# Banded attention feeding a token mixer on one core: a bias table multiplied in after exp, global keys batched over heads, and the attention of one batch interleaved with the mixing of another

## The chip, the core and the metric

The kernel runs on one core of one Trainium2 chip. The time is device microseconds (us) of one execution; a result is the median of several executions. The engines are PE (TensorE: matmuls and transposes), PEld (its weight loads, which overlap PE), DVE (VectorE), ACT (ScalarE: exp, sin and copies), POOL (GpSimd, which here also issues the input DMAs) and SP (which issues the output DMAs). Slow executions (over 1.5% above the fastest of the same kernel) are in the medians and ranges below, but not in the ratios. A verdict against the kernel before is a ratio: the mean time of one kernel's fast runs over the mean of the other's fast runs of the same rounds on the same chip. It is therefore not quite the ratio of the medians that are quoted beside it.

## The reference

There are 4 batches, 8 heads, 768 positions, head size 64. Attention is banded: a query sees the 96 keys up to and including its own position, and the first 8 keys of the sequence ("global keys"). A linear distance penalty is added to the scores. Then a token mixer works on the 768 x 512 result of each batch.

```python
# attention, for each batch b and head h
scores = q @ k.T / sqrt(64)
rel    = pos_q - pos_k
local  = (rel >= 0) & (rel < 96)
glob   = pos_k < 8
dist   = where(glob & ~local, 96, abs(rel))
scores = where(local | glob, scores - slope[h] * dist, -1e9)
x[b, :, h*64:(h+1)*64] = softmax(scores) @ v

# mixer, for each batch (x is 768 x 512)
theta = x @ w_theta                                    # "theta stretch"
y = w_tok_r @ (x * cos(theta)) + w_tok_i @ (x * sin(theta))   # "mixing"
u = x + y
out = u + relu(u @ w_ch)                               # "channel"
```

Mixing is the largest piece. It is 72 matmuls of 512 columns a batch; theta and channel are 24 each.

## The kernel before

Scores are computed transposed, keys on the partitions, in blocks of 128 keys by 256 queries, so exp gives directly what the value matmul needs as its stationary operand. The softmax sum comes from a column of ones beside v. The distance penalty and the mask are put into PSUM by a matmul of the identity with a bias table, and the scores are accumulated on top. Each head pair's q is copied into two tiles that are zero in the other head's 64 rows, so that a full 128-row matmul gives one head's scores.

```python
qTz_pool = [...]                       # per head of a pair: [128, 768], other head's rows zeroed
# per head:
for pair_i, jts in enumerate(((0, 1), (2, 3), (4, 5))):
    nc.tensor.matmul(ps_sc[...], lhsT=ident, rhs=biasM_all[h][:, b0:b0 + ncols, :],   # L195
                     start=True, stop=False)
    for sub, jt in enumerate(jts):
        nc.tensor.matmul(ps_sc[:, sub, 0:n * T], lhsT=kT2[:, jt * T:(jt + 1) * T],     # L203
                         rhs=qTz[:, its[0] * T:(its[-1] + 1) * T], start=False, ...)
nc.tensor.matmul(ps_gl[0:NG, :], lhsT=kT2[:, 0:NG], rhs=qTz[:, 2 * T:S], ...)          # L210 global keys
# [...]
nc.scalar.activation(exp_sb[...], ps_scs[hh][pair_i][...], AF.Exp, scale=scale)        # L220
nc.scalar.activation(eg[0:NG, :], ps_gls[hh][0:NG, :], AF.Exp, scale=scale, bias=...)  # L227
# [...] value matmuls L243: 128 x 128 by 128 x 65
```

The order of work leaves two batches of mixing for the end:

```python
for b in (0, 1):                       # attention alone
    # [...] attention_pair(b, 0), (b, 2), (b, 4), (b, 6), with the weight set-up in batch 0
for b in (2, 3):                       # attention of b beside the mixer of b - 2
    attention_pair(b, 0); moe_stage1(b - 2)            # theta
    attention_pair(b, 2); moe_stage2(b - 2, (0, 1, 2)) # mixing, L289
    attention_pair(b, 4); moe_stage2(b - 2, (3, 4, 5))
    attention_pair(b, 6); moe_stage3(b - 2)            # channel, L308
moe_stage1(2); moe_stage1(3); moe_stage2(2, ...); moe_stage2(3, ...)   # [...] the last two, alone
```

The softmax here doesn't subtract the row's maximum and nothing guards it: scores larger than these inputs give would overflow.

Of the kernel before, what the change touches and what calls it, by code (L numbers as in the profile page):

```python
# [9 lines left out]
FP = mybir.dt.float32  # L11
# [6 lines left out]
def kernel(  # L18
# [18 lines left out]
    NC = DM // T  # L37
    NG = int(n_global)
    NL = int(n_local)
    scale = 1.0 / math.sqrt(D)  # L40
    INF = 30000.0
    slopes = [2.0 ** (-8.0 * (h + 1) / H) for h in range(H)]
    HALF_PI = math.pi / 2.0

    const = ctx.enter_context(tc.tile_pool(name="const", bufs=1))
    xpool = ctx.enter_context(tc.tile_pool(name="xpool", bufs=2))
    abuf = ctx.enter_context(tc.tile_pool(name="abuf", bufs=3))
    mbuf = ctx.enter_context(tc.tile_pool(name="mbuf", bufs=2))
    psum = ctx.enter_context(tc.tile_pool(name="psum", bufs=8, space=bass.MemoryType.PSUM))

    def ps_tile(shape, dtype):
        return psum.tile(shape, dtype, name="ps", tag="ps")

    blk = {}
    nblk = 0
    for jt in range(NT):
        for it in ([0, 1] if jt == 0 else [i_ for i_ in (jt, jt + 1) if i_ < NT]):
            blk[(jt, it)] = nblk
            nblk += 1
# [3 lines left out]
    prefetch_requests = [(0, 0), (0, 2)]  # L63

    bias_glob = const.tile([T, H], FP)
    for h in range(H):
        nc.gpsimd.memset(bias_glob[:, h:h + 1], -float(NL) * slopes[h])
    halfpi = const.tile([T, 1], FP)
    nc.gpsimd.memset(halfpi, HALF_PI)

    dist_diag = const.tile([T, T], FP)
    nc.gpsimd.iota(dist_diag, pattern=[[1, T]], base=0, channel_multiplier=-1,
                   allow_small_or_imprecise_dtypes=True)
    nc.gpsimd.affine_select(dist_diag, dist_diag, pattern=[[1, T]], base=0,
                            channel_multiplier=-1, compare_op=ALU.is_ge, fill=INF)
    nc.gpsimd.affine_select(dist_diag, dist_diag, pattern=[[-1, T]], base=NL - 1,
                            channel_multiplier=1, compare_op=ALU.is_ge, fill=INF)

    dist_super = const.tile([T, T], FP)
    nc.gpsimd.iota(dist_super, pattern=[[1, T]], base=T, channel_multiplier=-1,  # L80
                   allow_small_or_imprecise_dtypes=True)
    nc.gpsimd.affine_select(dist_super, dist_super, pattern=[[-1, T]], base=NL - 1 - T,
                            channel_multiplier=1, compare_op=ALU.is_ge, fill=INF)

    g_row = const.tile([T, T], FP)
    nc.gpsimd.memset(g_row, float(NL))
    nc.gpsimd.affine_select(g_row, g_row, pattern=[[0, T]], base=NG - 1,
                            channel_multiplier=-1, compare_op=ALU.is_ge, fill=INF)

    dist_diag0 = const.tile([T, T], FP)  # L90
    nc.vector.tensor_tensor(dist_diag0, dist_diag, g_row, op=ALU.min)
    dist_super0 = const.tile([T, T], FP)
    nc.vector.tensor_tensor(dist_super0, dist_super, g_row, op=ALU.min)

    biasM_all = []
    for h in range(H):
        e_t = const.tile([T, 11, T], BF, name=f"biasM_all_{h}")
        f = -slopes[h] / scale
        nc.scalar.mul(e_t[:, 0, :], dist_diag0, f)
        nc.scalar.mul(e_t[:, 1, :], dist_super0, f)  # L100
        nc.scalar.mul(e_t[:, 2:11:2, :], dist_diag[:, None, :].to_broadcast([T, 5, T]), f)
        nc.scalar.mul(e_t[:, 3:10:2, :], dist_super[:, None, :].to_broadcast([T, 4, T]), f)
        biasM_all.append(e_t)

    eg_tiles = []
    for i_ in range(4):
        egt = const.tile([T, 4 * T], BF, name=f"eg_{i_}")
        nc.vector.memset(egt, 0.0)
        eg_tiles.append(egt)
    eg_cnt = [0]  # L110

    qTz_pool = [[], []]
    for hh in range(2):
        for i_ in range(3):
            t_ = const.tile([T, S], BF, name=f"qTz_{hh}_{i_}")
            nc.vector.memset(t_, 0.0)
            qTz_pool[hh].append(t_)
    qTz_cnt = [0, 0]

    w_theta_bf = const.tile([T, NC, DM], BF)  # L120
    w_ch_bf = const.tile([T, NC, DM], BF)
    w_tokT = [const.tile([T, NT, S], BF, name=f"w_tokT_{wi}") for wi in range(2)]
    w_nats = {}

    def setup_wsmall():
        nc.gpsimd.dma_start(out=w_theta_bf, in_=moe_w_theta.rearrange("(c p) n -> p c n", p=T))
        nc.gpsimd.dma_start(out=w_ch_bf, in_=moe_w_ch.rearrange("(c p) n -> p c n", p=T))
        for wi, w_src in enumerate((moe_w_tok_r, moe_w_tok_i)):
            w_nat = mbuf.tile([T, NT, S], BF, name="w_nat", bufs=2)
            nc.gpsimd.dma_start(out=w_nat, in_=w_src.rearrange("(c p) n -> p c n", p=T))  # L130
            w_nats[wi] = w_nat

    def setup_wtok(wi):
        w_nat = w_nats[wi]
        wT = w_tokT[wi]
        for st in range(NT):
            ps_tr = ps_tile([T, S], BF)
            for tt in range(NT):
                nc.tensor.transpose(ps_tr[:, tt * T:(tt + 1) * T],
                                    w_nat[:, tt, st * T:(st + 1) * T], ident)  # L140
            nc.vector.tensor_copy(out=wT[:, st, :], in_=ps_tr)

    x_sb = {}

    def load_pair(b, h0):
        qp = abuf.tile([T, NT, 2 * D], BF, name="qp")
        kp = abuf.tile([T, NT, 2 * D], BF, name="kp")
        for src, dst in ((q, qp), (k, kp)):
            for hh in range(2):
                nc.gpsimd.dma_start(  # L150
                    out=dst[:, :, hh * D:(hh + 1) * D],
                    in_=src[b, h0 + hh].rearrange("(t p) d -> p t d", p=T))
        v1s = []
        for hh in range(2):
            v1 = abuf.tile([T, NT, D + 1], BF, name=f"v1_{hh}")
            nc.gpsimd.dma_start(out=v1[:, :, 0:D],
                                in_=v[b, h0 + hh].rearrange("(t p) d -> p t d", p=T))
            nc.gpsimd.memset(v1[:, :, D:D + 1], 1.0)
            v1s.append(v1)
        return qp, kp, v1s  # L160

    preloaded = {}

    def attention_pair(b, h0):
        if (b, h0) in preloaded:
            qp, kp, v1s = preloaded.pop((b, h0))
        else:
            qp, kp, v1s = load_pair(b, h0)

        ps_q = ps_tile([T, S], BF)  # L170
        ps_k = ps_tile([T, S], BF)
        for src, pst in ((qp, ps_q), (kp, ps_k)):
            for t_ in range(NT):
                nc.tensor.transpose(pst[:, t_ * T:(t_ + 1) * T], src[:, t_, :], ident)  # L174
        qTzs = []
        for hh in range(2):
            t_ = qTz_pool[hh][qTz_cnt[hh] % 3]
            qTz_cnt[hh] += 1
            R = slice(D * hh, D * (hh + 1))
            nc.vector.tensor_copy(out=t_[R, :], in_=ps_q[R, :])  # L180
            qTzs.append(t_)
        kT2 = abuf.tile([T, S], BF, name="kT2")
        nc.scalar.copy(out=kT2, in_=ps_k)

        exp_sbs, ps_scs, ps_gls, egs = [], [], [], []
        for hh in range(2):
            h = h0 + hh
            qTz = qTzs[hh]
            exp_sbs.append(abuf.tile([T, 11, T], BF, name="exp_sb"))
            banks = []  # L190
            for pair_i, jts in enumerate(((0, 1), (2, 3), (4, 5))):
                ncols = 4 if pair_i < 2 else 3
                b0 = blk[(jts[0], 0 if jts[0] == 0 else jts[0])]
                ps_sc = ps_tile([T, 2, 2 * T], FP)
                nc.tensor.matmul(  # L195
                    ps_sc.rearrange("p a b -> p (a b)")[:, 0:ncols * T],
                    lhsT=ident,
                    rhs=biasM_all[h][:, b0:b0 + ncols, :].rearrange("p a b -> p (a b)"),
                    start=True, stop=False)
                for sub, jt in enumerate(jts):  # L200
                    its = [0, 1] if jt == 0 else [i_ for i_ in (jt, jt + 1) if i_ < NT]
                    n = len(its)
                    nc.tensor.matmul(ps_sc[:, sub, 0:n * T],  # L203
                                     lhsT=kT2[:, jt * T:(jt + 1) * T],
                                     rhs=qTz[:, its[0] * T:(its[-1] + 1) * T],
                                     start=False, stop=(sub == len(jts) - 1))
                banks.append(ps_sc)
# [23 lines left out]
        for hh in range(2):  # L231
# [3 lines left out]
            for it in range(NT):  # L235
                mms = []
                if it >= 2:
                    mms.append((eg[:, (it - 2) * T:(it - 1) * T], v1[:, 0, :]))
# [80 lines left out]
    for b in (0, 1):  # L319
        x_sb[b] = xpool.tile([T, NT, DM], BF, name="x_sb", bufs=4)  # L320
        attention_pair(b, 0)
        if b == 0:
            setup_wsmall()
# [61 lines left out]
```

## Time and profile before

Before the prediction the time was 255.59 us (254.84 to 257.77, 3 runs).

| | before |
|---|---|
| span of the profiled run | 255.4 us |
| PE busy, idle | 208.8 us, 46.6 us (the difference) |
| DVE, ACT, POOL busy | 114.9, 121.8, 87.7 us |
| share of PE in the chain of waits | 55% |

From the profile page of the kernel before: the span, the busy time of each engine, PE's busy tenths in 40 equal slices (6.4 us each), and the shares of the chain of work that ended last.

```profile
span 255.4 us, 4349 instructions
PE 208.8 (82%) x1712; PEld 118.7 (46%) x1736; DVE 114.9 (45%) x248; ACT 121.8 (48%) x230; POOL 87.7 (34%) x154
PE   0439819899868949999999759999999999999950
PE 55%; DMA 12%; POOL 9%; ACT 9%; DVE 8%; issue 5%; DVEq 0%; POOLq 0%; ACTq 0%
```

PE is nearly full from the middle on. It is thin in the first twelve slices, has a dip where theta is computed (the "75" in the middle is one), and is empty in the last slice.

The busy time of each engine by stretch of time (start:end, length, then busy time and number of instructions of PE, PEld, DVE, ACT and POOL, the granted clock, DMA share and GB/s):

```profile
82.00:94.00 12.00, 8.22 (x76) 4.88 (x75) 8.34 (x20) 8.61 (x15) 9.73 (x15) 1.00 1.25 80
138.00:149.00 11.00, 7.27 (x56) 3.98 (x57) 7.80 (x20) 8.14 (x14) 1.27 (x4) 1.00 0.62 62
201.00:232.00 31.00, 30.84 (x143) 14.06 (x144) 11.82 (x22) 5.26 (x10) 0.00 (x0) 1.00 0.00 1
```

The first two are theta stretches of batches 0 and 1: PE is busy 8.2 of 12 and 7.3 of 11 us. The third is mixing of the last two batches, alone: PE is full, and the other engines have little to do. That is the room that the change wants to use.

Groups of instructions before (line, engine, operation, output and inputs, shapes, count, then busy time and mean ns of one, then idle time before them):

```profile
L289 PE MATMUL ps<-zri,w_tokT_170 128*128 128x512 bf16 x142 | 53.8, 379 | 0.3
L220 ACT ACTIVATE exp_sb<-ps 128x512 bf16<-128x512 f32 x64 | 34.3, 583 | 10.0 <-PE ps L203 9.9
L273 DVE TENSOR_TENSOR zri<-x_sb,cs 128x512 bf16<-128x512 bf16 x24 | 10.1, 421 | 5.3 <-ACT cs L271 5.1
```

The 379 ns of a mixing matmul is the duration of one; matmuls overlap in the pipeline. What one costs in a row is read from the chain of waits, which gives start, length and count:

```profile
208.18 10.74 PE ps L289 x49
```

That is 10.74 / 49 = 0.219 us for a matmul of 512 columns.

### The profile page before, as it was taken

The page shows a single profiled execution, that of the slowest core. Times are in us where ns is not written, and L with a number is a line of the kernel's source. Part 1 is how long each engine was busy: PE and PEld are TensorE (multiplying, and loading weights), DVE is VectorE, ACT ScalarE, POOL GpSimd, SP SyncE. Part 2 cuts the span into 40 slices and gives each one's busy share as a digit, 9 for nine tenths or more (in the row PEclk, how much of TensorE's full clock was granted, in tenths as well). Part 3 has the DMA queues.
Part 4 walks back from the last instruction along what each step waited for, and adds up shares of the span by engine and source line. Part 5 has one row for each costly group of instructions (what it writes and reads, how often), then busy time and mean ns, then how long its engine had stood idle before and what let it go on. Part 6 is the DMA issues. An engine that isn't in the chain of part 4 may idle for free.

```text
span 255.4 us, 4349 instructions
## 1 busy us (share of the span) xinstructions
PE 208.8 (82%) x1712; PEld 118.7 (46%) x1736; DVE 114.9 (45%) x248; ACT 121.8 (48%) x230; POOL 87.7 (34%) x154
## 2 busy tenths in 40 slices
PE   0439819899868949999999759999999999999950
PEld 0216616666646525454646325555655444445520
DVE  5103432555423562323566533333678752325742
ACT  6985607598858585161618792332609730000000
POOL 9985128959566675571625000000000000000000
PEclk9999988999989997999999979999999999999995
DMA  4999999999899996993959300000042000000444
GB/s 27 115 129 195 211 163 92 110 87 99 55 77 85 92 84 41 92 74 21 78 141 197 22 0 0 3 0 0 3 166 85 0 0 0 3 0 0 164 167 164
DMA packets 81364, 19.42 MB, mean 76 GB/s; under 512 B 75712, under 2 KB 78272, under 8 KB 81344
## 3 DMA queue, kind: packets, MB, share of 16 engines
q0 software_dynamic: 77888, 12.85, 66.4%
q1 hardware_dynamic: 3456, 6.29, 6.7%
q8 instruction: 14, 0.23, 0.4%
q14 instruction: 6, 0.05, 0.1%
HBM read 25.69 MB, written 6.29 MB: 125 GB/s over the span
## 4 chain that ended last, share of the span: by engine, by line
PE 55%; DMA 12%; POOL 9%; ACT 9%; DVE 8%; issue 5%; DVEq 0%; POOLq 0%; ACTq 0%
PE ps L289 24%; PE ps L267 8%; DMA kp<-in_k_dram 7%; PE ps L203 5%; PE ps L243 4%; DMA out_dram<-o_sb 4%; ACT exp_sb L220 4%; PE ps L308 4%; PE ps L195 3%; DVE o_sb L312 3%; POOL kp L150 3%; PE ps L174 3%; POOL qp L150 3%; PE ps L210 2%; DMA v_0_190<-in_v_dram 1%
## 5 line engine op out<-in xcount | busy, mean ns | idle before, releaser
L289 PE MATMUL ps<-zri,w_tokT_170 128*128 128x512 bf16 x142 | 53.8, 379 | 0.3
L289 PE MATMUL ps<-zri,w_tokT_171 128*128 128x512 bf16 x139 | 52.7, 379 | 0.1
L220 ACT ACTIVATE exp_sb<-ps 128x512 bf16<-128x512 f32 (+1 forms) x96 | 46.5, 550 | 10.0 <-PE ps L203 9.9
L250 DVE RECIPROCAL rec<-ps 128x6 f32<-128x6 f32 x32 | 6.2, 194 | 65.7 <-PE ps L243 65.5
L293 DVE TENSOR_TENSOR u<-x_sb,ps 128x512 bf16<-128x512 bf16 x24 | 16.5, 687 | 36.3 <-PE ps L289 34.4
L150 POOL DMA_DIRECT2D qp<-in_q_dram x32 | 26.6, 841 | 14.3 <-PE ps L174 4.7
L150 POOL DMA_DIRECT2D kp<-in_k_dram x32 | 27.0, 853 | 0.9 <-PE ps L174 0.4
L271 ACT ACTIVATE cs<-ps,halfpi 128x512 bf16<-128x512 f32 x24 | 16.9, 703 | 16.4 <-PE ps L267 14.2
L312 DVE SCALAR_TENSOR_TENSOR o_sb<-ps,u 128x512 f32<-128x512 f32 x24 | 16.1, 687 | 13.9 <-DMA out_dram<-o_sb 11.6
L267 PE MATMUL ps<-w_theta_bf,xT 128*128 128x512 bf16 x92 | 21.5, 379 | 0.6 <-DVE xT L262 0.3
L308 PE MATMUL ps<-w_ch_bf,uT 128*128 128x512 bf16 x92 | 21.4, 379 | 0.3
L289 PEld LDWEIGHTS <-w_tokT_170 128*128 128x128 bf16 x144 | 14.1, 98 | 16.1
L289 PEld LDWEIGHTS <-w_tokT_171 128*128 128x128 bf16 x144 | 14.1, 98 | 16.1
L243 PEld LDWEIGHTS <-exp_sb 128*128 128x128 bf16 x352 | 17.6, 100 | 8.3 <-ACT exp_sb L220 2.3
L251 DVE TENSOR_TENSOR x_sb<-ps,rec 128x384 bf16<-128x384 f32 x32 | 17.8, 555 | 0.9
L174 PE MATMUL ps<-ident,qp 128*128 128x128 bf16 x96 | 8.5, 228 | 11.7 <-DMA qp<-in_q_dram 11.7
L272 ACT ACTIVATE cs<-ps 128x512 bf16<-128x512 f32 x24 | 14.7, 614 | 0.0
L267 PEld LDWEIGHTS <-xT 128*128 128x128 bf16 x96 | 9.0, 98 | 11.3 <-DVE xT L262 2.2
L308 PEld LDWEIGHTS <-uT 128*128 128x128 bf16 x96 | 8.9, 98 | 11.0 <-DVE uT L303 1.9
L174 PEld LDWEIGHTS <-qp 128*128 128x128 bf16 x96 | 6.5, 102 | 13.5 <-issue 7.2
L273 DVE TENSOR_TENSOR zri<-x_sb,cs 128x512 bf16<-128x512 bf16 x24 | 10.1, 421 | 5.3 <-ACT cs L271 5.1
L195 PEld LDWEIGHTS <-ident 128*128 128x128 bf16 x96 | 9.4, 105 | 6.3 <-issue 4.6
(341 smaller groups left out, 348.8 us busy)
## 6 DMA issues: line engine op xcount, KB each, us to landing
out_dram<-o_sb SPq DMA_DIRECT2D x24, 256.0 KB, 2.0
qp<-in_q_dram POOLq DMA_DIRECT2D x32, 96.0 KB, 3.4
kp<-in_k_dram POOLq DMA_DIRECT2D x32, 96.0 KB, 3.4
w_nat<-in_moe_w_tok_r_dram POOLq DMA_DIRECT2D x1, 1152.0 KB, 13.2
w_nat<-in_moe_w_tok_i_dram POOLq DMA_DIRECT2D x1, 1152.0 KB, 18.1
w_theta_bf<-in_moe_w_theta_dram POOLq DMA_DIRECT2D x1, 512.0 KB, 7.5
w_ch_bf<-in_moe_w_ch_dram POOLq DMA_DIRECT2D x1, 512.0 KB, 8.5
v_0_178<-in_v_dram POOLq DMA_DIRECT2D x1, 96.0 KB, 3.6
```

Of the source, the lines that this page charges most:

```text
L150: nc.gpsimd.dma_start(out=dst[:, :, hh * D:(hh + 1) * D], in_=src[b, h0 + hh].rearrange("(t p) d -> p t d", p=T))
L174: nc.tensor.transpose(pst[:, t_ * T:(t_ + 1) * T], src[:, t_, :], ident)
L195: nc.tensor.matmul(ps_sc.rearrange("p a b -> p (a b)")[:, 0:ncols * T], lhsT=ident, rhs=biasM_all[h][:, b0:b0 + ncols, :].rearrange("p a b ...
L220: nc.scalar.activation(exp_sb[:, b0:b0 + ncols, :].rearrange("p a b -> p (a b)"), ps_scs[hh][pair_i].rearrange("p a b -> p (a b)")[:, 0:nc ...
L243: nc.tensor.matmul(po[:, it, :], lhsT=lhsT, rhs=rhs, start=(i_ == 0), stop=(i_ == len(mms) - 1))
L251: nc.vector.tensor_mul(x_sb[b][:, :, h * D:(h + 1) * D], po[:, :, 0:D], rec.to_broadcast([T, NT, D]))
L267: nc.tensor.matmul(ps_th, lhsT=xT[:, dc, st * T:(st + 1) * T], rhs=w_theta_bf[:, dc, :], start=(dc == 0), stop=(dc == NC - 1))
L271: nc.scalar.activation(cs[:, 0, :], ps_th, AF.Sin, bias=halfpi)
L289: nc.tensor.matmul(ps_y, lhsT=w_tokT[wi][:, st, tt * T:(tt + 1) * T], rhs=zri[:, st, wi, :], start=(n == 0), stop=(n == 2 * NT - 1))
L293: nc.vector.tensor_add(u[:, tt, :], xb[:, tt, :], ps_y)
L308: nc.tensor.matmul(ps_c, lhsT=uT[:, dc, st * T:(st + 1) * T], rhs=w_ch_bf[:, dc, :], start=(dc == 0), stop=(dc == NC - 1))
L312: nc.vector.scalar_tensor_tensor(o_sb, in0=ps_c, scalar=0.0, in1=u[:, st, :], op0=ALU.max, op1=ALU.add)
```

## The change

The intent: take the bias matmuls off PE (multiply by a table of exp(-slope * dist) after exp, on DVE), compute scores on the 64 rows that a head has, with no zero-padded copies of q and with 224 instead of 256 query columns, compute the global keys of all head pairs together, and put the attention of batch b+1 beside the mixing of batch b, so that only one batch mixes alone. Exp, sine and copy calls become fewer and larger.

The diff, cut to its core (names that only move are left out):

```diff
-        nc.scalar.mul(e_t[...], dist_..., f)                  # bias table, for an identity matmul
+    for h in range(H):                                        # table of factors, [128, 8, 224]
+        nc.scalar.activation(etab[:, h, :], dist, AF.Exp, scale=-slopes[h])
+    nc.gpsimd.affine_select(etab, ...)                        # twice: zero outside the band
 ...
-    load_pair(b, h0): q, k, v of two heads, 96 KB a DMA
+    load_v: nc.gpsimd.dma_start(out=vn[...], in_=v[b, h0:h0 + n]...)   # v of all 8 heads in one DMA
 ...
+    def globals_(b):
+        for hh in range(2):
+            pg = ps_big()
+            for p in range(NP):                               # four head pairs, 32 columns of the array each
+                for c0, c1 in ((0, 512), (512, S)):
+                    nc.tensor.matmul(pg[GS * p:GS * (p + 1), c0:c1], lhsT=kT[R, 0:GS],
+                                     rhs=qT[R, c0:c1], start=True, stop=True)
+            nc.scalar.activation(e_, pg[:, 0:S], AF.Exp, scale=scale, bias=gbias[:, hh:hh + 1])
+            nc.vector.tensor_mul(e_[:, 0:T], e_[:, 0:T], gmask)
 ...
+    def scores(b, p, c):
+        for j in range(2):
+            for hh in range(2):
+                R = slice(D * hh, D * (hh + 1))               # 64 rows: one head of the pair
+                nc.tensor.matmul(pb[:, hh, j * W:j * W + n], lhsT=kT[R, jt * T:(jt + 1) * T],
+                                 rhs=qT[R, jt * T:jt * T + n], start=True, stop=True)
+        nc.scalar.activation(e_t[:, :, jt:jt + 2, 0:W], pb[...], AF.Exp, scale=scale)
+        nc.vector.tensor_mul(e_t[:, :, jt:jt + 2, 0:W], e_t[:, :, jt:jt + 2, 0:W],
+                             etab[:, 2 * p:2 * p + 2, None, :].to_broadcast([T, 2, 2, W]))
 ...
+    def vglob(b, p):      # a small matmul with a shift matrix puts v's 8 global rows on the right partitions
+    def weave(main, side): # issues steps of `side` between steps of `main`, in proportion to their weights
 ...
+    for b in range(B):
+        nxt = b + 1 if b + 1 < B else None
+        # theta(b), then the q and k transposes of nxt
+        # main: mix(b), with utrans and chan of the row before; weight transposes in batch 0
+        weave(main, attention_steps(nxt) if nxt else [])
```

## The prediction

> **What bounds it now.** TensorE. The page's part 1 gives PE 208.8 of 255.4 us (82%), ACT 122, DVE 115, POOL 88; the chain of waits is 55% PE. Matmul durations overlap: in the chain, 49 mixing matmuls of 512 columns take 10.74 us, 219 ns each, not the group's 379. At such spacings (a transpose or 65-column matmul about 0.055 us) I estimate PE needs per batch: theta 5.2, mixing 15.6, channel 5.2, transposes 5.4, scores with bias and globals 11.2, values 6.6: 49 us; with weight transposes (4) 201 us in all. The other 55 are a thin start (stretches by window: PE 5.6 of the first 20 us, none in 32-36), theta waits (two stretches of 11-12 us around 82 and 138, PE busy 8.2 and 7.3), and a tail of evictions and output DMAs.
>
> **What changes.**
> - Removed: bias matmuls (1,408 columns a head, 0.6 us; 19 us in all), zero-padded q, eight global-key matmuls a batch. Scores run on 64-row halves, 224 instead of 256 columns. The Trainium skill, "TensorE: Matmul & The Clock Gate", Part 3, says such halves run concurrently; no instruction of this trace shows it. Estimate for scores and globals: 11.2 down to 4-8 us a batch.
> - Added: 16 value matmuls and 4 small ones a batch (1 us PE); DVE multiplies by the table: from 421 ns for 512 bf16 elements I estimate 0.6 us for 896, 6-7 us a batch. uT evictions move to ACT (3 us a batch); two table loads a batch, 1.28 us each.
> - ACT: fewer, larger calls. From 583 ns at 512 and 482 at 384, 896 elements cost about 0.89; exps fall from 18.5 to about 13 us a batch, sines from 7.9 to 6.4. ACT and DVE totals stay near 115-125 us, off the critical path.
> - Moved: attention of batch b+1 beside mixing of b. Only the last batch, not two, mixes alone.
>
> **Predicted course.** Loads of 96 KB take 0.82 us of POOL each. Batch 0 has 24 loads' worth, v last in one DMA behind table set-up, so its values start at 27-31 us (before: 22). Attention 0 is unwoven; two large PSUM buffers couple scores, exps and normalization, about 5 us a head pair; theta 0 starts at 45-51. Then three times theta with q/k transposes (10 us) plus woven mixing (36-38 us; 4 more the first time): 142-146. Last: theta, mixing, channel, tail: 35. Sum about **226 us**, range **212 to 242**. Faster by over 2%: 0.93, within 2%: 0.04, slower: 0.03.
>
> **On the critical path:** nearly all of the PE saving (4 x 4-7 us less 4 x 1), about 12 us of theta stalls, part of the overlap; against it the start, which waits longer for v.
>
> **What would show it.** Part 1: PE busy falls 15-30 us, ACT within 10, DVE up 0-15. Slices: PE low until about 28 us, then 9s from about 50 to near the end. Groups: score matmuls of the two halves start together, or not; table multiply 0.5-0.7 us; v's DMA issue 5-7 us on POOL. Theta stretch about 10 us. Waits: first value matmul released by v's DMA.
>
> **What would make it wrong.** The halves may not overlap, or switching between half and full array may drain it ("TensorEngine Tiling (Array Packing)", Key Properties, says so; no run shows it): 24 switches a batch at an estimated 0.1-0.2 us cost 10-20 us. Batch 1's loads, behind the weights, could stall theta 0. A faster v DMA gives under 215.

## The result and the profile after

The changed kernel took 218.53 us (218.5 to 218.86, 4 runs) against 256.19 us of the kernel before in the same rounds. The ratio is 0.8522, with a 95% interval of 0.8476 to 0.8567. All outputs are right. The prediction of 226 us (212 to 242) held, 7.5 us too high.

The same parts of the page, with the row of the granted clock, of the changed kernel (a slice is now 5.4 us):

```profile
span 217.1 us, 4192 instructions
PE 185.3 (85%) x1752; PEld 100.0 (46%) x1752; DVE 120.0 (55%) x242; ACT 112.3 (52%) x168; POOL 79.3 (37%) x107
PE   0486225978889999999999999999999999999981
PEclk9999999999999999999999999999999999999997
PE 70%; POOL 8%; ACT 8%; DVE 6%; DMA 5%; issue 2%; POOLq 0%; ACTq 0%
```

The span fell by 38.3 us. PE's busy time fell by 23.5 us. Its idle time fell from 46.6 to 31.8 us, by 14.8. So, by this split into busy and idle time, about three fifths of the gain are work taken off PE, and two fifths are gaps closed. The row of PE slices shows where the gaps were and what is left. The dips in the middle are gone, and what is left is at the start (the "6225") and in a short tail. The next row is the clock that the profile shows as granted; it is not to be trusted before 43.9 us, as is shown below. PE's share of the chain of waits rose from 55% to 70%.

By stretch of time, in the same columns as before. First the woven mixing of batch 1, then the theta stretch of batch 2 with the q and k transposes of batch 3:

```profile
107.20:139.70 32.50, 32.50 (x338) 16.56 (x338) 20.45 (x42) 19.14 (x32) 0.00 (x0) 1.00 0.09 34
139.70:149.00 9.30, 9.30 (x85) 5.71 (x82) 6.42 (x12) 8.08 (x9) 0.00 (x0) 1.00 0.16 59
```

PE has no gap in either (the next woven stretch, 149.00 to 181.55 us, is full too: 32.55 of 32.55). In the woven mixing DVE and ACT have a third and more of their time free. There PE work is what counts, and work moved to DVE or ACT costs nothing as long as PE does not come to wait for it (e3_padded_q below shows a place where it does).

The groups that answer to those above:

```profile
L322 PE MATMUL ps<-zri,w_tokT_162 128*128 128x512 bf16 x144 | 54.6, 380 | 0.5 <-DVE zri L312 0.4
L241 ACT ACTIVATE e_156<-pb 128x896 bf16<-128x896 f32 x8 | 7.3, 917 | 7.7 <-PE pb L237 7.7
L244 DVE TENSOR_TENSOR e_156<-e_156,etab 128x896 bf16<-128x896 bf16 x8 | 5.0, 624 | 6.5 <-ACT e_156 L241 6.5
```

Mixing is what it was. An exp of 896 elements takes 917 ns and a multiplication by the table 624 ns; the prediction had 0.89 and 0.6 us. The Trainium skill, "ScalarE: Activation LUTs", section "What ACT_TABLE_LOAD costs", gives 186 ns plus 0.833 ns an element for a call with immediate scale and bias. That makes an estimate of 932 ns for 896 elements, with which the trace's 917 ns agrees.

Inside the woven stretch, PE's instructions in order of time (start, length, line; a length overlaps the next start):

```profile
108.71 0.38 PE L322 MATMUL ps<-zri,w_tokT_163 128*128 128x512 bf16 x1
109.02 0.36 PE L237 MATMUL pb<-qT,kT 64*128 64x224 bf16 x4
109.32 0.39 PE L322 MATMUL ps<-zri,w_tokT_162 128*128 128x512 bf16 x1
...
112.66 0.38 PE L322 MATMUL ps<-zri,w_tokT_162 128*128 128x512 bf16 x1
112.97 0.52 PE L215 MATMUL pb<-qT,kT 64*32 64x512 bf16 x8
113.42 0.39 PE L322 MATMUL ps<-zri,w_tokT_163 128*128 128x512 bf16 x1
```

Two mixing matmuls in a row start 0.22 us apart. Here the score block starts 0.31 us after the mixing matmul before it, so 0.09 us of gap comes first, and the next mixing matmul starts 0.30 us after the block. Four matmuls of 224 columns, one after the other, would be 4 x 224/512 x 0.219 = 0.38 us, so the two row halves do run at the same time (the packed trace has the two heads' matmuls start 3 ns apart, the next two 103 ns later), but not twice as fast: with the gap the block costs 0.39 us. The Trainium skill says both things: "TensorE: Matmul & The Clock Gate", Part 3, that row tiles run concurrently, and "TensorEngine Tiling (Array Packing)", Key Properties, that "Changing tiling mode (not just tile) drains the TensorE". This trace puts a number on the second: two concurrent pairs would be 0.19 us, and the block costs 0.39, so about 0.2 us goes with each visit to the 64-row mode. One sign of what it is: between mixing matmuls a weight load starts one matmul ahead, 0.22 us, but the first load of this block starts at 109.016 us, 4 ns before its matmul. The eight global matmuls (3,072 columns, 1.31 us one after the other at that rate) take 0.45 us and the gap: there it pays that four column groups run at once.

The start, from the chain of waits:

```profile
18.66 10.31 DMA vn<-in_v_dram
33.40 0.56 DVE gmask L150
33.98 0.23 DVE eg_317 L219
34.26 2.00 PE pb L279 x33
```

v of batch 0 is issued by POOL at 18.66 us, after all q and k loads and the table set-up, and takes 10.3 us to land. Then the mask for the global keys, which stands behind other work in DVE's queue, holds the value matmuls until 34.26 us (a single one had started at 31.40). The work that it stands behind waits for v too: on ACT the two copies of v's global rows, which need v, come at 29.32 us, before the exps of the global keys. And those 33 values take 2.00 us. Woven ones in the same trace take half of that for each:

```profile
117.84 0.52 PE pb L279 x17
```

The Trainium skill, "TensorE: Matmul & The Clock Gate", Part 1, says that TensorE starts at half its clock and gets the full one only after some 3.4 us of sustained activity. By their start times the first values stand 55 ns apart and the woven ones 30, which agrees with it, and experiments below test it. The records of the clock in the packed trace say why the row of 9s hides this: the first one starts at 43.92 us (full clock), there is none before it, and the page prints a 9 where there is none. The spacing of the values changes from 55 to 30 ns at 43.9 us. The trace of before has its first record at 23.25 us and then four stretches of 3.41 us at half clock, from 36.9, 74.5, 94.9 and 149.5 us, besides the tail; the changed kernel has none between 43.9 us and its tail. Taking the time before the first record as half clock, PE is busy at half clock for 21.8 us in either trace, outside the tail, so the clock does not distort the comparison of busy times.

### The profile page after: what moved, and what is told of

It is laid out like the page before. It is cut to its first block, busy times and chain, and to the rows that moved or that the text cites. A ratio compares the mean times of both kernels' runs of the same rounds, so it can differ in the third digit from the quotient of the medians.

```text
span 217.1 us, 4192 instructions
## 1 busy us (share of the span) xinstructions
PE 185.3 (85%) x1752; PEld 100.0 (46%) x1752; DVE 120.0 (55%) x242; ACT 112.3 (52%) x168; POOL 79.3 (37%) x107
## 4 chain that ended last, share of the span: by engine, by line
PE 70%; POOL 8%; ACT 8%; DVE 6%; DMA 5%; issue 2%; POOLq 0%; ACTq 0%
PE ps L322 29%; PE ps L341 10%; PE pb L279 8%; PE pb L305 7%; PE pb L237 5%; DMA vn<-in_v_dram 5%; POOL kn L73 3%; PE ps L332 3%; POOL qn L73 3%; PE ps L200 3%; PE ps L290 2%; DVE zri L312 1%; PE ps L182 1%; ACT cs L309 1%; ACT kT L204 1%
## 5 line engine op out<-in xcount | busy, mean ns | idle before, releaser
L334 ACT COPY uT<-ps 128x512 bf16<-128x512 bf16 x24 | 14.1, 588 | 39.4 <-PE ps L332 39.4
L73 POOL DMA_DIRECT2D qn<-in_q_dram x32 | 26.9, 879 | 11.3 <-DMA vn<-in_v_dram 7.3
L73 POOL DMA_DIRECT2D kn<-in_k_dram x32 | 26.6, 869 | 0.5 <-DMA qn<-in_q_dram 0.5
L305 PE MATMUL pb<-w_theta_bf,xT 128*128 128x512 bf16 x96 | 23.5, 379 | 0.0
L237 PE MATMUL pb<-qT,kT 64*128 64x224 bf16 x192 | 19.2, 277 | 3.8 <-ACT eg_317 L218 1.2
L202 DVE COPY qT<-ps 128x768 bf16<-128x768 bf16 x16 | 8.8, 555 | 17.8 <-PE ps L200 17.6
L204 ACT COPY kT<-ps 128x768 bf16<-128x768 bf16 x16 | 12.3, 831 | 9.7 <-PE ps L200 9.7
L312 DVE TENSOR_TENSOR zri<-x_sb,cs 128x1024 bf16<-128x1024 bf16 x24 | 16.0, 687 | 2.1 <-ACT cs L309 1.3
L309 ACT ACTIVATE cs<-pb,halfpi 128x1024 bf16<-128x1024 f32 x12 | 13.5, 1122 | 4.7 <-PE pb L305 4.6
L285 DVE TENSOR_TENSOR x_sb<-pb,rec 128x768 bf16<-128x768 f32 x16 | 15.3, 957 | 0.5
L310 ACT ACTIVATE cs<-pb 128x1024 bf16<-128x1024 f32 x12 | 12.4, 1029 | 0.0
## 6 DMA issues: line engine op xcount, KB each, us to landing
w_ch_bf<-in_moe_w_ch_dram POOLq DMA_DIRECT2D x1, 512.0 KB, 10.3
```

The lines of the kernel that those rows point to most:

```text
L73: nc.gpsimd.dma_start(out=dst[:, :, h * D:(h + 1) * D], in_=src[b, h].rearrange("(t p) d -> p t d", p=T))
L237: nc.tensor.matmul(pb[:, hh, j * W:j * W + n], lhsT=kT[R, jt * T:(jt + 1) * T], rhs=qT[R, jt * T:jt * T + n], start=True, stop=True)
L285: nc.vector.tensor_mul(xv, po4[:, :, :, 0:D], rec.to_broadcast([T, 2, NT, D]))
L305: nc.tensor.matmul(pb[:, j, :], lhsT=xT[:, dc, st * T:(st + 1) * T], rhs=w_theta_bf[:, dc, :], start=(dc == 0), stop=(dc == NC - 1))
L309: nc.scalar.activation(cs[:, 0], pb, AF.Sin, bias=halfpi)
L312: nc.vector.tensor_mul(zri[b][:, i_, 2 * c:2 * c + 2, :], xb[:, 2 * c:2 * c + 2, :], cs[:, i_])
```

## Experiments

The theory after the result (A) had these parts: each of the table, the weave and the batched globals removes PE time or PE gaps, with the half-row scores no more than a small part, and what is left to gain is at the start. The rivals (B) were that the table is worth nothing because DVE and ACT work takes its place, that the globals are not worth batching, and that the start is bound by loads whatever the clock.

| run | what it is | us, median (range) | ratio to before, 95% |
|---|---|---|---|
| after_again | the changed kernel again | 218.69 (218.5-221.38) | 0.8568 (0.8524-0.8613) |
| e1_no_weave | attention after mixing, not within it | 235.91 (235.11-240.17) | 0.9160 (0.9057-0.9264) |
| e2_bias_matmul | bias by matmul again | 228.68 (228.4-228.76) | 0.8887 (0.8796-0.8978) |
| e11_bias_no_weave | both of these | 244.18 (243.48-244.3) | 0.9498 (0.9458-0.9539) |
| e4_before_table | kernel before, with the table | 257.61 (255.8-257.92) | 1.000 (0.9905-1.0094) |
| e8_globals_apart | global keys pair by pair | 235.21 (233.56-241.01) | 0.9122 (0.9001-0.9243) |
| e3_padded_q | zero-padded q, full rows | 224.55 (224.34-225.31) | 0.8780 (0.8745-0.8815) |
| e9_sine_early | sine table loaded ahead | 219.96 (219.81-220.81) | 0.8572 (0.8539-0.8606) |
| e5_warm | 24 idle matmuls at the start | 216.22 (214.6-216.39) | 0.8439 (0.8402-0.8476) |
| e6_front | v and masks earlier | 213.15 (212.43-215.18) | 0.8352 (0.8307-0.8397) |
| e7_front_warm | both, and loads reordered | 212.03 (211.17-212.2) | 0.8245 (0.8215-0.8275) |
| e12_all | e7 with three more edits | 214.35 (212.7-215.1) | 0.8385 (0.8337-0.8433) |

The runs came in four groups, each on its own chip and with its own runs of the kernel before (258.34 us for e1, e2, e4 and e8; 255.37 for after_again, e3, e5 and e6; 256.69 for e7, e9 and e11; 255.63 for e12). Across groups I therefore compare ratios: the changed kernel has 0.8522 and 0.8568, mean 0.8545, and one hundredth is 2.56 us. The intervals of these runs reach 0.8 to 3.1 us to each side, so a difference between two groups is good to some 3 us. What is used below of e1, e2 and e8 is their distance from the changed kernel, 9 to 16 us, which is far outside that.

For the mechanism I also use the start of each theta (the first theta matmul of batches 0 to 3). In the changed kernel these are at 48.3, 91.8, 139.6 and 181.4 us, so the stretches between them are 43.5, 47.7 and 41.8 us. The end of the last stretch is the span. A first theta matmul can be issued well ahead of the rest: that of batch 1 stands 5.8 us ahead here (91.8, the next at 97.7), so the first stretch reads short by that and the second long. In the woven variants it is 5.8 to 6.2 us too, so the same stretches compare; without the weave it is 1.2 to 1.7. At theta 0 the first matmul stands 1.5 to 2.8 us ahead of where the rest run on (50.1 us in the changed kernel), so theta 0 is good to about 1 us between variants. (The expectation of e6_front, which has theta 0 at 50.3, counts from there.)

### The changed kernel once more

> The changed kernel unaltered, as the yardstick for the runs beside it on the same chip: 218 to 219 us by every theory.

No edit; it shared its rounds with some of the runs below. It took 218.69 us. Five of its six runs were at 218.5 to 219.7 us with a granted clock of 0.99; the profiled one was at 0.95 (its clock record has 0.949 from 41.4 us to the tail) and took 221.38. The stretches below are therefore compared with the first trace (0.994).

### Without the weave

```diff
-        weave(main, attention_steps(nxt) if nxt else [])
+        weave(main, [])
+        weave(attention_steps(nxt) if nxt else [], [])
```

> The changed kernel (218.5 us) with the attention of the next batch issued after token mixing instead of woven into it; the instruction order of TensorE confirms that it runs after. Theory A (TensorE-bound: in the woven stretches PE is busy all the time, and unwoven attention is bound by the latency between scores, exps and normalization): attention 0 took 21 us from v's arrival to theta, its PE work in a woven stretch is about 12 us, so each of three batches loses 4 to 9 us: 231 to 245 us. Rival B (the weave is worth nothing, all the gain is removed PE work): 217 to 222 us.

It took 235.91 us, a ratio higher by 0.0615: 15.7 us more than the changed kernel. By stretch, batch 1's theta, mixing alone, and then attention of batch 2 alone:

```profile
99.63:109.00 9.37, 8.38 (x87) 5.22 (x86) 5.75 (x13) 6.10 (x7) 2.52 (x2) 1.00 1.10 71
109.00:131.00 22.00, 21.85 (x134) 10.38 (x133) 9.98 (x17) 9.40 (x13) 0.00 (x0) 1.00 0.36 67
131.00:147.66 16.66, 12.56 (x205) 8.11 (x204) 11.63 (x26) 11.80 (x22) 0.00 (x0) 1.00 0.05 18
```

Attention alone leaves PE idle for 4.1 of 16.7 us. In the chain of waits of the whole run DVE has 14% and ACT 13%, where the changed kernel has 6 and 8%. The total PE busy time is nearly the same as in the changed kernel (186.8 against 185.3 us). So the weave is worth some 16 us, all of it gaps, as A said. By stretch, with batch 1's theta of the changed kernel taken at 97.7, the three that lost their weave grew by 2.3, 6.1 and 6.2 us, and the last one by 2.0.

### Bias by matmul again

```diff
-    etab: exp(-slope * dist), zero outside the band; tensor_mul after each exp
+    btab: -slope / scale * dist, with 30000 for dist outside the band
+        for hh in range(2):
+            nc.tensor.matmul(pb[:, hh, 0:2 * W], lhsT=ident,
+                             rhs=btab[:, 2 * p + hh, None, :].to_broadcast([T, 2, W]),
+                             start=True, stop=False)
```

> The changed kernel with the bias put back as a matmul against the identity (two of 448 columns for each block of scores) and the table multiplies on VectorE taken out. Theory A (PE-bound in the woven stretches): 24 matmuls a batch of 448 columns at about 0.19 us each are 4.5 us of PE, 13 to 15 us in three woven batches and 0 to 4 us in the unwoven first: 231 to 238 us, while VectorE's busy time falls by about 27 us. Rival B (removed PE work hardly counts, VectorE and latency matter as much): 214 to 222 us.

It took 228.68 us, a ratio higher by 0.0342: 8.8 us more. That is between the two expectations; A had put it too high. From its woven stretch:

```profile
115.80 0.54 PE L233 MATMUL pb<-btab,ident 128*128 128x448 bf16 x2
116.27 0.36 PE L241 MATMUL pb<-qT,kT 64*128 64x224 bf16 x4
```

A block's two bias matmuls take 0.47 us up to the start of the scores. Their columns alone (896) would be 0.38 us; twelve blocks a batch would be 4.6 us. The last stretch between two thetas grew from 41.8 to 46.2 us, by 4.4. DVE's busy time fell from 120.0 to 94.4 us, and that gave nothing back, since DVE had room. In this kernel the table is thus worth about 9 us. That is a net figure: the edit also puts the masks on the small distance tile, as e6_front does below, so v is issued at 15.94 instead of 18.66 us and theta 0 comes 1.8 us earlier. From theta 0 to the end this run takes 180.5 us against 168.9, so without that help at the start it would have lost nearer 11 us, by estimate.

### Both

```diff
 e2_bias_matmul, and in it:
-        weave(main, attention_steps(nxt) if nxt else [])
+        weave(main, [])
+        weave(attention_steps(nxt) if nxt else [], [])
```

> Both undone: the weave (as in e1, 235.9 us) and the table (bias matmuls back, as in e2, 228.7 us, which was 10 us slower than the changed kernel's 218.6). Theory A (removed PE work pays only where TensorE is the limit, as e4 says, where the table alone gained nothing): without the weave the bias matmuls cost little, 0 to 5 us over e1: 235 to 241 us. Rival B (parts add up): 10 us over e1, 245 to 248 us.

The two could have depended on each other: without the weave PE waits, and matmuls that fill waits cost nothing. It took 244.18 us, a ratio of 0.9498: 24.4 us more than the changed kernel, where 15.7 and 8.8 add up to 24.5. So the two effects add, within the 3 us that such a comparison is good to (both runs with the bias matmuls have the earlier v). My theory that most of the table's value needs the weave falls. That the table also shortens the attention's own chain, where the bias matmul precedes each score block, is a likely reason; it was not shown by itself.

### The table in the kernel before

```diff
-        nc.scalar.mul(e_t[...], dist..., -slopes[h] / scale)
+        nc.scalar.activation(e_t[...], dist..., AF.Exp, scale=-slopes[h])
-                nc.tensor.matmul(ps_sc[...], lhsT=ident, rhs=biasM_all[h][...], start=True, stop=False)
+            # after each exp:
+                nc.vector.tensor_mul(exp_sb[:, b0:b0 + ncols, :], exp_sb[:, b0:b0 + ncols, :],
+                                     biasM_all[h][:, b0:b0 + ncols, :])
```

> The kernel before (256 us) with that one part of the change alone: its bias matmuls out, a multiply of the exps by a table on VectorE in (96 multiplies of 384 or 512 elements, 0.35 to 0.42 us each). PE loses 19 us of work, VectorE gains about 35 us. Theory A (PE-bound nearly everywhere): 238 to 248 us. Rival B (the overlap is what counts; before, attention is bound by latency through ACT and DVE): 252 to 260 us.

It took 257.61 us, a ratio of 1.000: B held. From its page:

```profile
PE 195.8 (77%) x1625; PEld 112.4 (44%) x1640; DVE 146.9 (58%) x344; ACT 121.5 (48%) x230; POOL 88.1 (35%) x154
PE 49%; ACT 16%; DMA 12%; DVE 12%; POOL 5%; issue 3%; DVEq 0%; POOLq 0%; ACTq 0%
```

PE lost 13.0 us of busy time, and the time did not move, within the 2.4 us of the interval. The chain of waits says where it went: PE's share fell from 55 to 49%, ACT's rose from 9 to 16 and DVE's from 8 to 12. In the old structure a head pair's period in batch 1, before any mixing, is about 5.2 us with the bias matmuls and about 5.25 with the table (successive starts of the pairs' q transposes). There DVE also has padded q copies, and got 32 us more. So "PE work removed" was worth 9 us in one structure and nothing in the other. What of this is DVE's load and what is the order of issue was not separated. A third part may be the clock: after its first record this trace has 20.5 us at half clock outside the tail, the kernel before 13.7.

### Global keys pair by pair

```diff
         for hh in range(2):
-            pg = ps_big()
             for p in range(NP):
+                pg = ps_big()
                 # the same matmuls for this pair
-            nc.scalar.activation(e_, pg[:, 0:S], AF.Exp, ...)
+                nc.scalar.activation(e_[G, :], pg[G, 0:S], AF.Exp, ...)    # 32 partitions each
```

> The changed kernel with the global keys of the four head pairs no longer batched: each pair's scores in a PSUM tile of its own and an exp of 32 partitions each, 8 exps of about 0.93 us a batch instead of 2. Theory A (PE-bound; ACT has 40% of a woven stretch free): ACT rises by about 22 us of busy time in all, the time by 0 to 5 us, most of it in the first, unwoven batch: 218 to 224 us. Rival B (batching the global keys is a main part of the gain): over 226 us.

It took 235.21 us, a ratio higher by 0.0577: 14.8 us more than the changed kernel. B held, and by more than I had thought possible. From its woven stretch:

```profile
120.41 0.39 PE L324 MATMUL ps<-zri,w_tokT 128*128 128x512 bf16 x1
120.72 0.49 PE L216 MATMUL pb<-qT,kT 64*32 64x512 bf16 x2
121.15 0.60 PE L324 MATMUL ps<-zri,w_tokT 128*128 128x512 bf16 x2
```

Two matmuls of one pair take 0.43 us, and 0.09 of gap, 0.52 in all; eight in the batched form take 0.45. Eight visits a batch are 4.2 us against 2 x 0.54 = 1.1. That is 3.1 of the 4.2 us by which the last stretch grew (46.0 against 41.8). Exp over 32 partitions costs as much as over 128 (892 ns each in the list of groups, against 892 to 952 ns), so 32 calls in place of 8 add 21.8 us of ACT (134.1 against 112.3). And the first values come 5.6 us later (37.0 against 31.4 us), of which 1.9 us are left at theta 0 (50.2). The three stretches after it grew by 5.1, 4.2 and 4.2 us.

### Zero-padded q

```diff
-                nc.vector.tensor_copy(out=dst, in_=ps)
+                for hh in range(2):
+                    nc.vector.tensor_copy(out=dst[hh][R, :], in_=ps[R, :])   # other 64 rows are zero
-                nc.tensor.matmul(pb[...], lhsT=kT[R, ...], rhs=qT[R, ...], ...)
+                nc.tensor.matmul(pb[...], lhsT=kT[:, ...], rhs=qT[hh][:, ...], ...)
+    # [...] the global keys likewise; q and k buffers 4 each instead of 6
```

> The changed kernel with q put into two zero-padded copies, so that scores and global keys use all 128 rows, one head after the other, as in the kernel before. Theory A (the halves' gain is eaten by switching): in a woven stretch a block of four score matmuls on half rows took 0.39 us of PE, of which 0.19 is what two concurrent pairs of 224 columns need and 0.2 comes with the change of rows; on full rows the four need 4 x 0.093 = 0.37 us and no switch, so the time moves by -2 to +2 us: 216.5 to 220.5 us, with the gap before a block gone. Rival B (the concurrency of the halves is worth its 0.19 us in each of 48 blocks): 9 us more, 225 to 230 us. VectorE's busy time rises by about 9 us by either.

It took 224.55 us, 5.9 more than the changed kernel in the same rounds, and neither theory had that. From its timeline of PE, and from its list of waits (who waited for whom; total us, times, longest):

```profile
112.91 2.98 PE L332 MATMUL ps<-zri,w_tokT 128*128 128x512 bf16 x13 [1.09 <-DVE qz L212]
...
121.58 0.55 PE L247 MATMUL pb<-qz,kT 128*128 128x224 bf16 x4
121.97 1.03 PE L332 MATMUL ps<-zri,w_tokT 128*128 128x512 bf16 x4
...
PE ps L208 <- DVE qz L212: 3.4, 5, 1.3
```

A full-row score block takes 0.39 us, the same as the half-row block with its gap. So on PE the two forms are equal here, and the overlap of the halves only pays for the change of mode. The loss is elsewhere. Theta 0 came 0.9 us later, and the stretches after it were 2.3, 1.9 and 1.2 us longer. PE's busy time did not grow in any of them (39.8, 46.7 and 41.5 us against 41.1, 47.6 and 41.8); its idle time did. In the second, PE waits 2.0 us in all for DVE's q copies; the first line above is one of these waits. In the third, the woven part is not longer (31.8 against 32.4 us from first mixing to next theta), but from the end of theta to the first mixing matmul it takes 3.75 us instead of 2.0; there PE stands 0.62 us for a q copy at 154.04 us and 0.20 for a k copy, and one more score block comes before mixing. DVE was busy 132.9 instead of 120.0 us. So what the half rows gave here is, for the most part, one copy in place of two: the waits show it for the second stretch and for a part of the third, and I take it to be so for the first (1.8 us of such waits, beside 2.2 for DVE's copies of the weights). That DVE held a copy back for want of one of the fewer q buffers is not seen where I looked: at 152.8 and 155.7 us it goes from one copy to the next without a pause. A rival would be the clock, since these runs are listed at a granted 0.95 and those of the changed kernel at 0.99. The traces rule it out: this one has a record of half clock from 23.3 to 43.8 us, where the other has no record and runs at the same half clock, and both are at full clock from 43.9 to the tail.

### The sine table ahead

```diff
+    def early_sine(b):      # after the last exps and values: a sine of one element
+        nc.scalar.activation(sdum, ebuf[(b, NP - 1)][:, 1, NT - 1, 0:1], AF.Sin)
```

> The changed kernel with a one-element sine right after the last exp of each batch, so that the sine table is loaded while ACT is idle (it sat idle 4.8 us before the last uT copy, then copied 0.6 us and loaded 1.28 us while TensorE had theta's first chunk ready). Theory A (that load lies on the critical path of every theta stretch but the first): 1.3 us in each of three or four stretches, 213.5 to 216 us. Rival B (as the prediction has it, theta stretches are bound by TensorE and ACT work, loads don't matter): 218 to 219 us.

It took 219.96 us with a ratio of 0.8572, which is that of the changed kernel (0.8545 for its two measurements, 0.8568 for the later one). So no gain is to be seen, and A, which had expected one, failed; B had 218 to 219, and the 1 us above it is less than a comparison between groups is good to. ACT's timeline shows that the table load went where it was meant to, into idle time:

```profile
136.31 0.59 ACT L335 COPY uT<-ps 128x512 bf16<-128x512 bf16 x1 [0.21 <-PE ps L333]
136.91 1.28 ACT L356 ACT_TABLE_LOAD   x1
138.20 0.20 ACT L356 ACTIVATE sdum<-e 128x1 f32<-128x1 bf16 x1
```

But in this version the scheduler put all theta work of the batch ahead of the q and k transposes, and the k copies came later. From theta 3 to the end it took 34.9 instead of 35.7 us (no attention follows there); the two stretches before were 1.4 and 1.2 us longer than in the first trace. These are small differences of single traces, and the run does not tell the cost of the load by itself: it is inconclusive on that.

### Warm matmuls at the start

```diff
+    def warm(b, p, n):
+        ps = ps_small([T, 512], FP)
+        for i_ in range(n):
+            nc.tensor.matmul(ps, lhsT=ident, rhs=kT[:, 0:512], start=True, stop=True)
...
     for p in range(NP): prep(0, p)
+    warm(0, NP - 1, 24)
```

> The changed kernel with 24 matmuls of 512 columns, their result unused, in the idle time of TensorE before v arrives. Theory A (TensorE runs slowly in the first 44 us because it was idle before: value matmuls are spaced 0.060 us there and 0.030 later): with them the value matmuls of the first batch are spaced near 0.03 from the start, and the time falls by 1.5 to 5 us: 213.5 to 217 us. Rival B (the spacing there is set by weight loads or waits, or the first batch is bound by ACT, DVE and their latency): 217.5 to 219.5 us.

Twenty-four matmuls, whose result nobody reads, keep PE busy from 23 to 30 us, while it would have waited for v. It took 216.22 us, 2.5 less in the same rounds. Theta 0 moved from 48.3 to 45.1 us, or, where its matmuls run on, from 50.1 to 47.8. The value matmuls were at 30 ns for the first part of the way, and at 55 ns again from about 33.9 us for a time, so the gain was not complete. The clock records agree with the spacing: full from 26.82 us, half from 33.65, full again from 40.48.

### v and the masks earlier

```diff
-    load_v(0, 0, 8)                          # before the set-up of the global masks
-    nc.gpsimd.affine_select(etab, ...)       # twice, on [128, 8, 224], after the exps
+    nc.gpsimd.affine_select(dist, ...)       # twice, on [128, 224], before the exps; fill 30000
-    nc.gpsimd.memset(shift / gtmp / gmk / gmk2, 1.0)
+    nc.vector.memset(shift / gtmp / gmk / gmk2, 1.0)
-    # [...] an iota and a memset whose results are not needed
+    for p in range(NP):
+        load_v(0, 2 * p, 2)                  # after that set-up, four loads by head pair
```

> The changed kernel with only its start altered: v of the first batch in four loads by head pair, table masks put on the distance before the exp (3 us less of POOL), global-key masks set up before v's loads. Theory A (the start is bound by the loads: the first values wait for v's landing at 29.0 us and the mask until 34.3): values start at 23 to 27 us, theta 0 at 40 to 45 instead of 50.3; but batch 1's keys land at about 46 to 48, so a part is lost to waiting before the third theta chunk: 210 to 216 us. Rival B (the start is bound by the chain through PSUM, not the loads): 217 to 219 us.

It took 213.15 us, 5.5 less. The first value matmul moved from 31.4 to 23.3 us (the run of them from 34.3 to 24.4) and theta 0 to 38.9, 9.4 us earlier. But the next stretch grew from 43.5 to 46.8 us, so about a third of the gain was given back there. Batch 1's loads stand in the queue behind the same token weights and do not come earlier with the rest. The trace shows that they are most of the cause: in this stretch PE waits three times, 2.9 us in all, for the DMA of batch 1's keys, and in the changed kernel not at all.

### Both, with another order of loads

```diff
 e6_front, and:
+    warm(0, NP - 1, 16)
-    w_theta, all token weights, w_ch; then all of batch 1
+    w_theta, token weights of row 0, q and k of batch 1, rows 1-2, v of batch 1, the rest, w_ch
```

> The start of e6_front (213.2 us) with 16 warming matmuls before the first values and batch 1's q and k loaded ahead of five sixths of the token weights. Theory A (both effects are real and, as in e6, theta 0 runs into waiting for batch 1's keys: its stretch from first theta to next theta was 46.8 us there against 43.5): values of batch 0 spaced at 0.03 us, theta 0 starts at 36 to 38 us, the stretch falls back to 44 to 45.5: 208.5 to 211.5 us. Rival B (the start is now bound by the loads' total, reordering only moves the wait to the token weights): 212 to 215 us.

It took 212.03 us, the fastest kernel: 17.6% less than the kernel before and about 3% less than the changed one. Its first values:

```profile
21.64 4.02 PE L231 MATMUL ps<-kT,ident 128*128 128x512 bf16 x14 [0.22 <-issue]
...
27.86 0.19 PE L289 MATMUL pb<-vn,e 128*128 128x65 bf16 x1 [0.42 <-ACT eg L221]
```

The values now run at 30 ns from the first on, but the sixteen matmuls push the first one from 23.3 to 27.86 us, and theta 0 is at 38.8, no earlier than without them. (Where its matmuls run on it is 41.6 us, against 40.7 without.) What it gains over e6_front (1.1 us by the medians, 2.7 by the ratios; the two were in different groups) goes with the stretch after theta 0 (45.6 instead of 46.8), the one that the order of loads should shorten: PE's waits for the keys of batch 1 are gone from its list.

### The warming spread, and two more

```diff
 e7_front_warm, and:
-    warm(0, NP - 1, 16)
+    if p < NP - 1: warm(0, p, (4, 3, 3)[p])   # after each pair's transposes
+    # the global-key v matmuls wait for the global exps (a zero multiple of these is written into `shift`)
+    # early_sine for the last batch only
```

> The load order and mask order of the version with 16 warming matmuls (212.0 us), but the warming matmuls are spread: 4, 3 and 3 of them after the first three head pairs' transposes, none after the last; the vglob matmuls are made to wait for the global exps so that the scheduler cannot put them ahead; and the last batch's sine table is loaded early. Theory A (what is left of the start is the serial path from the last q/k load to the first values, which the 16 warming matmuls lengthened by 4 us): first value matmul at 23-25 us instead of 27.9 and at the 0.03 us spacing, theta 0 at 36-37 instead of 38.8, last stretch 0.9 us shorter: 208-211 us. Theory B (the start is bound by the loads and by what scores, exps and normalization take in turn): theta 0 stays near 38.5, 211-213 us.

It took 214.35 us: neither theory, and slower than e7_front_warm. Theta 0 came at 42.6 us, and the early sine did not shorten the last stretch by the 0.9 us hoped for (35.3 against 35.5). The start, on PE and on DVE:

```profile
22.97 0.80 PE L204 MATMUL ps<-ident,kn 128*128 128x128 bf16 x6 [4.49 <-DVE qT L206]
...
18.22 0.16 DVE L124 TENSOR_REDUCE gsel<-gtmp 128x1 f32<-128x4 f32 x1 [4.93 <-POOL gtmp L122]
...
22.37 0.55 DVE L206 COPY qT<-ps 128x768 bf16<-128x768 bf16 x1
```

In this version the mask set-up stands ahead of the last two q copies in DVE's queue; which of the edits moved it was not tested. DVE stood from 13.3 to 18.2 us, the next q copy came at 22.4 us, and PE stood for 4.5 us until that copy was done (probably for the PSUM buffer that it frees). In that wait the clock fell back (its record turns from full to half at 22.61 us): the granted clock was 0.63 between 20 and 30 us and 0.69 between 30 and 40, and the values ran at 55 ns. The run does not test its theory; it shows that here one gap of 4.5 us in the start went with the loss of the clock until 36.3 us.

## Why the prediction was right, and where it was off

- **What bounds it: right.** PE's busy time was predicted to fall by 15 to 30 us and fell by 23.5. ACT was to stay within 10 and fell by 9.5; DVE was to rise by 0 to 15 and rose by 5.1.
- **Course of the stretches: right but for one, and one of them by luck.** Start 45 to 51 us: theta 0 was at 48.3. But two errors cancel in it: the values ran from 34.3 us, later than the 27 to 31 foreseen, and the four head pairs then took 14.0 us, 3.5 each and not 5. Theta with transposes 10: measured 9.3 to 9.4. Last batch 35: measured 35.7. The weight transposes were put at 4 us; the first two stretches together take 91.2 us against 2 x 41.8, so they and the stall at the first theta cost about 7.6. The slices were to be 9s from about 50 us; they are so from about 65.
- **The mis-sized term: "woven mixing (36-38 us ...)", built on "a transpose or 65-column matmul about 0.055 us".** The woven stretch took 32.5 us. A value matmul costs 31 ns there, so a batch's values take 8 x 0.52 = 4.2 us, where 0.055 us each makes 7.5. That is 3.3 us a batch, 10 us over three batches, and most of the 12 us by which the three stretches together came in low (133.1 us from theta 0 to theta 3, against the 145 that the prediction's numbers add up to). The wrong number could have been seen in the trace of before. Its value matmuls stand 55 ns apart at 98.1 us and 31 ns apart at 98.4 us, a moment later, with the same shape:

```profile
98.02 0.30 PE L243 MATMUL ps<-v_0_1331,exp_sb 128*128 128x65 bf16 x2
98.13 0.25 PE L243 MATMUL ps<-v_0_1331,eg_152 128*128 128x65 bf16 x1
...
98.34 0.23 PE L243 MATMUL ps<-v_0_1331,exp_sb 128*128 128x65 bf16 x2
98.41 0.19 PE L243 MATMUL ps<-v_0_1331,eg_152 128*128 128x65 bf16 x1
```

  (Two instructions in 0.11 us, then two in 0.07.) The first is the half clock: this trace has a clock record, and it turns from half to full at 98.34 us. Transposes really take 56 ns at the full clock (18 of them in 1.00 us at 81.80 us of the same trace), and one number was used for both.
- **Scores on half rows, 4 to 8 us a batch with globals: right in size** (12 x 0.39 + 2 x 0.54 = 5.8), the two halves do start together (3 ns apart), and the fear about the change of mode was right too: at about 0.2 us a visit it takes nearly all that the overlap gives. e3_padded_q shows equal block times.
- **v's DMA: half right.** The issue took 2.3 us on POOL, not the 5 to 7 that the prediction looked for. But the load did hold the first values, since it was issued last and took 10.3 us to land; then DVE's mask held them.
- **Parts of the gain, by removing them one at a time:** weave 16 us, table 9, batched globals 15 (against a pair-by-pair form that is not that of the kernel before), half rows with one q copy for two 6. These are not shares: they sum to 46 us, more than the 38 gained. Weave and table add up; the others were not tried together with them. Without weave and table the ratio is 0.9498, still 13 us below the kernel before, and how these 13 divide among the other edits was not separated.

## What to carry to other kernels

Before work is taken off the busiest engine, see whether that engine is full in the stretch, and try it: the same table was worth 9 us here and nothing in a structure where the chain of waits went over to ACT and DVE. Read the cost of a small matmul from a stretch where PE has been busy for several us, and check it against the number of columns, since at the half clock a value matmul stood at 55 ns here instead of 30. Do not take a full mean clock for a full clock at the start: ask whether the trace has a record there. When the middle is full, look at the start: the order in which loads and mask set-up are issued was worth another 2.5% (e6_front), and an edit there must be read back from each in-order queue, because a scheduler may answer it by moving something else, as in e12_all.

## What the Trainium skill lacked or had wrong

- "TensorEngine Tiling (Array Packing)", Key Properties, says that a change of mode drains TensorE but gives no time. Here each visit to the 64-row mode among full-array matmuls costs about 0.2 us (0.39 us for a block whose two concurrent pairs would be 0.19; that this is the drain is our reading), enough to make half-row scores in blocks of four no faster than zero-padded ones (0.39 us).
- "TensorE: Matmul & The Clock Gate", Part 3, describes the concurrency of small tiles, but not what it is worth when they are scattered: eight global matmuls in four column groups take 0.45 us together, and the two of one head pair, one after the other in one group, take 0.43 us alone.
- The same page's Part 1 was right, and it warns that clock events in a trace have been seen to be unreliable. It does not say how the half clock came to be hidden here: the trace of the changed kernel has no clock record before 43.92 us, and its profile page prints full clock where there is none, while the values at 34 to 36 us stand 55 ns apart instead of 30. The spacing of equal matmuls was the safer sign; from the first record on, spacing and records agree.
- "ScalarE: Activation LUTs", What ACT_TABLE_LOAD costs, gives about 1,283 ns for the load, which every load here takes, and about 1,380 ns of drain with it, 2.66 us in all. The trace does not show that drain: in e9_sine_early the copy before the load ends at 136.90 us, the load starts at 136.91, and the sine starts at 138.20, 1.3 us in all.
